# Turning q, k and x by DMA from chunk 14 instead of 18, with new planning numbers

## The chip, the cores and the metric

The kernel runs on one core of a Trainium2 chip. The metric is the time of one execution in microseconds (us) on the device. The core has TensorE (PE: matmuls; PEld: its weight loads), VectorE (DVE), ScalarE (ACT), GpSimd (POOL) and SyncE (SP, which here only issues DMAs), and 16 DMA engines that carry all transfers.

## What is computed

Gated linear attention runs over 4 batches x 8 heads x 768 steps with a head dimension of 48, and its output, as 3072 tokens of 384, goes through a two-layer MLP with a squared ReLU:

```python
for t in range(S):
    state = alpha[:, :, t, :, None] * state + np.einsum('bhd,bhe->bhde', k[:, :, t], v[:, :, t])
    y[:, :, t] = np.einsum('bhd,bhde->bhe', q[:, :, t], state)
...
h = x @ w_in
r = np.maximum(h, 0.0)
g = r * r
return (g @ w_out).astype(np.float32)
```

Inputs and outputs are float32; the kernel multiplies in bf16. w_in is 384 x 2048, w_out 2048 x 384.

## The kernel before, in words

The recurrence is cut into 24 chunks of 128 steps, 6 for each batch. For each chunk (`add_chunk`, from line 421) the kernel

- loads alpha, q, k and v (`at`, `qt`, `kt`, `vt`; line 362, on SP's queue, 192 KB each);
- takes logs of alpha (line 431, ACT), sums them along the chunk by a matmul with a triangular matrix, and exponentiates the sums: `A` or `Af` (line 459) and `Ainv` (line 463);
- multiplies q by A and k by 1/A (lines 487 to 493, DVE) into `qk_s`, which has four places, one for every fourth chunk;
- turns both, so that the head dimension lies on partitions: `qkT`;
- computes scores `sc` from `qkT`, masks them into `sm` (line 561), adds what comes from the state (`bank<-sb,qkT`) and from the chunk itself (`bank<-vb,sm`), and updates the state `st` (`st<-vb,qk_s`, then line 595);
- copies its output to bf16 (`xn`, line 388, ACT) and turns it into `xT_big`, the input of the MLP's first layer.

The first four chunks go through a version of their own (`add_super`). From chunk 8 on the scores of two chunks (8/9, 10/11, ...) are computed together.

There are two ways to turn. Up to a chunk `XFROM` (18) TensorE transposes: 8 matmuls with an identity for q and k and 3 for x (all line 269), into PSUM banks that the attention shares with the scores and the outputs; DVE then copies the result out (line 390, as `qkT` and `xT_big`; a few of the early ones go to ACT). From `XFROM` on SP issues one DMA transpose for q and k together (line 507, 256 KB with its padding) and one for x (line 409), from SBUF to SBUF. From chunk `TURN` (12) on, the chunk's decay factor `ae` (`ae_s`) is not computed by ACT, but taken from the last row of `Af` by two small DMAs that POOL issues (line 476).

The MLP works on groups of 4, 1, 1 and then 2 chunks (groups 6, 7 and 8 are the chunks 12/13, 14/15 and 16/17). The first layer (`bank<-xT_big,w_in_b`) is 16 x 3 matmuls for a group, with ReLU on ACT (line 866) and the square on DVE (line 874, `gT`); the second (`bank<-w_out_b,gT`) is 16 matmuls for each chunk. Results are copied out as `ob` (line 938) and stored on POOL's queue (line 947), those of the last three chunks on SP's.

The order of all this is written out by a planner in the file (`Plan`, line 63) when the program is built. Each piece of work is an `Op` with an engine, an assumed duration, a latency `lat` until its result may be used, and the pieces that it waits for; `Plan.run` lets time pass, each engine takes the piece that can start first (among equals the one with the lower `prio`), and the pieces are emitted sorted by planned start. Each engine then executes its list in just this order on the chip, and waits, by semaphores, where a result is not there yet. The planned times appear nowhere in the program, only the order does.

Four details of the planner matter here. A matmul that depends on another engine gets 0.05 us of slack after it, and 0.25 after planned time 25. Loads (engine "DMA") are planned first in, first out, with a duration and a latency of 2.4. From planned time `ISSUE_AT` on, everything that SP issues (loads, DMA transposes "XB", stores "OUT") also takes SP's time, 0.6 us or 1.25 for a transpose. And a gate holds a chunk's first matmul back until the MLP has come within `LEAD` (3.5) chunks of it; from chunk 12 on the lead grows by a quarter of a chunk per chunk, to 5.

Of the kernel before, what the change touches and what calls it, by code (L numbers as in the profile page):

```python
# [33 lines left out]
LAT = {"PE": 0.13, "ACT": 0.14, "DVE": 0.13, "POOL": 0.25}  # L34
PE_SLACK = 0.05
ISSUE = {"DMA": 0.6, "OUT": 0.6, "SPD": 1.2, "XB": 1.25}
ISSUE_AT = 75.0
PE_CALM = 25.0
PAUSES = [(13.0, 1.0), (18.0, 1.0)]

# [18 lines left out]
def after(op, x=0.0):  # L59
    return (op, x)  # L60


class Plan:
# [37 lines left out]
    def run(self, gate):  # L101
        free = self.free
        while any(self.pending.values()):
            best = None
            for eng, ops in self.pending.items():
                t0 = free.get(eng, 0.0)
                pick = None
                fifo = eng in ("DMA",)
                for op in (ops[:1] if fifo else ops):
                    if not gate(op):  # L110
                        continue
                    r = self.ready(op)
                    if r is None:
                        continue
                    if len(op.durs) > 1:
                        ends = {e: max(r, free.get(e, 0.0)) + x + LAT[e] for e, x in op.durs.items()}
                        if ends[eng] > min(ends.values()):
                            continue
                    key = (max(r, t0), op.prio)
                    if pick is None or key < pick[0]:  # L120
                        pick = (key, op)
                if pick is not None and (best is None or pick[0][0] < best[0]):
                    best = (pick[0][0], eng, pick[1])
            assert best is not None, "nothing can run"
            t, eng, op = best
            for e in op.durs:
                self.pending[e].remove(op)
            op.eng, op.dur = eng, op.durs[eng]
            op.start = t + getattr(op, "late", 0.0)
            if eng == "DMA" and self.pauses and t >= self.pauses[0][0]:  # L130
                op.dur += self.pauses.pop(0)[1]
            free[eng] = t + op.dur
            if op.lat is None:
                op.lat = LAT.get(eng, 0.2)
            if hasattr(op, "hold"):
                free["DMA"] = max(free.get("DMA", 0.0), t) + op.hold
            if hasattr(op, "dma"):
                free["DMA"] = max(free.get("DMA", 0.0), t) + op.dma
            if eng == "OUT":
                free["DMA"] = max(free.get("DMA", 0.0), t) + op.dur  # L140
            op.done = t + op.dur + op.lat
            if eng in ISSUE and t >= ISSUE_AT:
                sp = max(free.get("SPQ", 0.0), t)
                free["SPQ"] = sp + ISSUE[eng]
                op.start = max(op.start, sp)
                op.done = max(op.done, sp + ISSUE[eng] + op.lat)
                if eng == "DMA":
                    free[eng] = sp + op.dur
                    op.done = sp + op.dur + op.lat
            if op.takes is not None:  # L150
                self.ready(op)
                op.slot.release.append(op.gives if op.gives is not None else op)
            self.order.append(op)
            self.on_pick(op)
        self.order.sort(key=lambda o: o.start)
# [3 lines left out]
def kernel(  # L159
# [21 lines left out]
    NT = n_tok // P  # L181
# [64 lines left out]

    NBUF = 4
    TURN = 12
    AE_LAT = 3.0
    L_s = big.tile([P, NBUF, H, DP], BF16)  # L250
    nc.gpsimd.memset(L_s[:, :, :, D:], 0.0)
    qk_s = big.tile([P, NBUF, 2, H, DP], BF16)
# [9 lines left out]
    def pin(ins):  # L262
        tc.keep_in_program_order(ins)
# [4 lines left out]
    def tr(*a):  # L268
        pin(nc.tensor.transpose(*a))  # L269
# [11 lines left out]
    def psum(op, shape, dt):  # L281
        i = op.slot.bank
        return banks[i].tile(shape, dt, name=f"bank{i}")
    X_SLACK = 0.2
    LD = 1.05
# [4 lines left out]
    def add(eng, dur, emit, *deps, **kw):  # L290
        return plan.add(Op(eng, dur, emit, deps, **kw))
# [47 lines left out]
    SRC = dict(srcs)  # L339
    EARLY = 2 * 3  # L340
    PAIRS = 8
    XFROM, XTO = 18, NT
    XLAT = 2.8
    LEAD = 3.5

    NS = 2
# [6 lines left out]
    def add_load(s, nm):  # L353
        d = C[s]
        b, c = divmod(s, NCH)
        k = s // 2

        def ld():
            if s % 2 == 0:
                PAIR[k][nm] = loads.tile([P, 2, H, D], FP32, name=nm)  # L360
            d[nm] = PAIR[k][nm][:, s % 2]
            pin(nc.sync.dma_start(out=d[nm], in_=SRC[nm][b, c]))
        prev = C[s - LB]["use_" + nm] if s - LB >= 2 * NS else None
        if 2 * NS <= s < 2 * NS + LB and (k - LB // 2) < NS:
            prev = SUP[k - LB // 2]["use_" + nm]
        pace = C[s - LB + 1]["use_" + nm] if s >= TURN + 2 else None
        d["ld_" + nm] = add("DMA", LD if s < TURN else 0.97, ld, prev, pace, lat=2.4)

    PAIR = [dict() for _ in range(NT // 2)]
    SRC2 = [("at", alpha), ("qt", q), ("kt", k), ("vt", v)]  # L370
# [15 lines left out]
    def cast(op, out_t, in_t):  # L386
        if op.eng == "ACT":
            pin(nc.scalar.copy(out_t, in_t))  # L388
        elif op.eng == "DVE":
            pin(nc.vector.tensor_copy(out_t, in_t))  # L390
        else:
            pin(nc.gpsimd.tensor_copy(out_t, in_t))

    def add_tail(s, done, first, g):
        d = C[s]

        def e_xn():
            d["xn"] = work.tile([P, HD], BF16, name="xn")
            cast(xn, d["xn"], d["py"][:, 0:HD])
        xn = add("ACT", 0.36, e_xn, done, **g)  # L400
        first.gives = xn

        def e_p4():
            d["px"] = psum(p4, [P, KT, P], BF16)
            for j in range(KT):
                tr(d["px"][:, j, :], d["xn"][:, j * P:(j + 1) * P], ident_bf)
        if XFROM <= s < XTO:
            def e_xturn():
                pin(nc.sync.dma_start_transpose(out=xT_big[:, :, s * P:(s + 1) * P], in_=d["xn"]))
            d["x"] = add("XB", 0.0, e_xturn, xn, lat=XLAT - 0.9)  # L410
            d["end"] = xn
            return
        p4 = plan.add(Op("PE", 0.165, e_p4, [xn], takes=GLA_BANKS, lat=0.14, **g))

        def e_xT():
            cast(xT, xT_big[:, :, s * P:(s + 1) * P], d["px"])
        xT = add({"ACT": 0.36, "DVE": 0.27} if s < EARLY else "DVE", 0.27, e_xT, p4, prio=-9.0)
        d["x"] = d["end"] = xT
        p4.gives = xT

    def add_chunk(s):
        d = C[s]
# [48 lines left out]
        a_ = add("ACT", 0.38 if s < TURN else 0.76, e_A, p0, **g)  # L471
# [5 lines left out]
        if s < TURN:  # L477
            ae0 = add("ACT", 0.18, e_ae0, p0, after(ai), **g)
            p0.gives = ae1 = add("ACT", 0.19, e_ae1, p0, after(ae0), **g)
        else:  # L480
            p0.gives = ai
            ae1 = add("POOL", 1.8, e_aed, a_, lat=AE_LAT, prio=-20.0)
            ae1.dma = 0.3

        def e_qA():
# [26 lines left out]
        def e_cp(lo, hi):  # L512
            if lo == 0:
                d["qkT"] = work.tile([P, 2 * NP, P], BF16, name="qkT")
            cast(cpk if lo else cp, d["qkT"][:, lo:hi, :], d["pT"][:, lo:hi, :])
        if s < EARLY:
            cp = add({"ACT": 0.49, "DVE": 0.34}, 0, lambda: e_cp(0, NP), p1q, **g)
            cpk = add({"DVE": 0.34, "ACT": 0.49}, 0, lambda: e_cp(NP, 2 * NP), p1k, after(cp, -9.0), **g)
        elif s < XFROM:
            cp = cpk = add("DVE", 0.61, lambda: e_cp(0, 2 * NP), p1k, **g)  # L520
        else:
            cp = cpk = add("XB", 0.0, e_turn, mq, mk, lat=XLAT)
        if s < XFROM:
            p1q.gives = cpk

# [46 lines left out]
    def add_back(s):  # L572
# [47 lines left out]
        p3b = plan.add(Op("PE", 0.21, e_p3b, [after(sm1, 0.02), sm0, vb, after(p3a)], takes=None if c else GLA_BANKS, lat=0.15, **g))  # L620

        add_tail(s, p3b, p3a or p3b, g)

    def add_super(u):
# [209 lines left out]
    OUT_AT = 72.0  # L834
# [6 lines left out]
    prog = {"m1": 0.0, "m2": 0.0}  # L841
# [69 lines left out]
    def add_moe2(g, tt, before, box, quarters, pools):  # L911
# [3 lines left out]
        for qd in quarters:  # L915
# [8 lines left out]
            op = plan.add(Op("PE", 0.65, e_mm, deps, takes=pools if qd == 0 else None, prio=0.1))  # L924
# [14 lines left out]
        ev = add({"DVE": 0.47, "ACT": 0.38}, 0, e_ev, op, prio=-15.0)  # L939
        box["first"].gives = ev  # L940

        s = GT[g] + tt
# [6 lines left out]
                for t in range(2):  # L949
                    pin(q.dma_start(out=out2_r[s, t], in_=box["ob"][HF * t:HF * t + HF]))  # L950
        if s < NT - 3:
            add("POOL", 1.0, e_out, ev, at=OUT_AT + 3.0 * s, lat=2.5, prio=5.0).dma = 0.55
        else:
            add("OUT", 0.55, e_out, ev)
        return op
# [37 lines left out]
    def gate(op):  # L993
        s = getattr(op, "gla", None)
        if s is not None:
            return s <= (LEAD if s < 12 else min(5.0, LEAD + 0.25 * (s - 11))) + (prog["m1"] + prog["m2"]) / 5.12
        return True

    def on_pick(op):
        m = getattr(op, "moe", None)  # L1000
        if m:
            prog["m1" if m[0] == 1 else "m2"] += m[1]
    plan.on_pick = on_pick
    plan.run(gate)


# [47 lines left out]
```

## Time and profile before

| what | value |
| --- | --- |
| median of 3 runs | 181.76 us (181.5 to 182.21) |
| profiled execution, time | 181.87 us |
| profiled execution, span | 180.1 us |
| granted TensorE clock | 1.000 |
| scores of pairs 12/13, 14/15, 16/17, 18/19 start at | 92.2, 105.4, 115.6, 129.0 us |
| first-layer matmuls of groups 6, 7, 8, 9 start at | 98.5, 111.8, 122.2, 137.3 us |
| last matmul ends at | 177.4 us |

The span runs from the first to the last instruction that the profiler recorded; the execution's time is 1.8 us longer. All positions in this document are us from the start of the span. In a row of the profile a tile is written out<-in, with buffer numbers left out. The start of a DMA is the start of its issue, and "to landing" counts from there to the semaphore that tells of its end. A matmul's record lasts longer than the step from one matmul to the next, since they are pipelined; a piece of the chain counts the steps.

### The profile page before, as it was taken

What the parts mean: (1) busy time and instruction counts of PE and PEld (TensorE: products, weight loads), DVE (VectorE), ACT (ScalarE), POOL (GpSimd) and SP (SyncE); (2) the same over time, 40 slices, a digit from 0 to 9 for tenths busy, and PEclk for the clock granted to TensorE, in tenths of its full rate; (3) what the DMA queues carried; (4) which work ended last, traced back from release to release, by engine and by line L of the source; (5) the groups of instructions that cost most, each with busy time, mean ns of one, the idle gap of its engine ahead of it and who ended that gap; (6) DMA issues with size and microseconds to landing.
All of it is one profiled execution on the core that took longest, in us unless ns stands there. A gap on an engine that the chain in (4) does not pass through costs nothing.

```text
span 180.1 us, 4934 instructions
## 1 busy us (share of the span) xinstructions
PE 174.0 (97%) x1926; PEld 129.4 (72%) x1927; DVE 130.3 (72%) x269; ACT 122.4 (68%) x260; POOL 54.2 (30%) x95
## 2 busy tenths in 40 slices
PE   7799999999999999999999999999999999999993
PEld 3467684566996788866877887878767866868663
DVE  6699669847799889885999897997864971724300
ACT  4556879357997598937685967889577863657421
POOL 6023466612111116503643504543245022011100
PEclk9999999999999999999999999999999999999999
DMA  5999999999998989989999694596276325031022
GB/s 141 274 277 321 323 356 378 214 211 215 189 202 166 224 172 232 289 185 214 198 273 278 151 223 109 132 195 155 54 106 155 77 44 146 5 87 44 4 87 87
DMA packets 107799, 32.39 MB, mean 180 GB/s; under 512 B 101840, under 2 KB 106064, under 8 KB 107776
## 3 DMA queue, kind: packets, MB, share of 16 engines
q1 hardware_dynamic: 105536, 27.93, 70.3%
q0 software_dynamic: 2240, 4.15, 6.5%
q8 instruction: 15, 0.25, 0.6%
q14 instruction: 8, 0.07, 0.1%
HBM read 25.17 MB, written 4.72 MB: 166 GB/s over the span
## 4 chain that ended last, share of the span: by engine, by line
PE 87%; DVE 4%; ACT 3%; DMA 2%; issue 2%; SPq 1%; ACTq 0%; DVEq 0%
PE bank L266 77%; PE bank L269 5%; DMA at<-in_alpha_dram 2%; PE sc L266 2%; PE st L266 2%; ACT r L866 2%; DVE qkT L390 1%; DVE sm L753 1%; SPq L383 1%; DVE qk_s L690 1%; ACT xn L388 0%; DVE xT_big L390 0%; DVE qk_s L487 0%; ACT L_s L638 0%; ACT A L674 0%
## 5 line engine op out<-in xcount | busy, mean ns | idle before, releaser
L266 PE MATMUL bank<-xT_big,w_in_b 128*128 128x256 bf16 (+2 forms) x599 | 72.5, 268 | 0.2
L266 PE MATMUL bank<-w_out_b,gT 128*128 128x384 bf16 (+2 forms) x400 | 70.4, 319 | 0.0
L866 ACT ACTIVATE r<-bank 128x512 bf16<-128x512 f32 x96 | 56.8, 607 | 12.6 <-PE bank L266 10.4
L266 PEld LDWEIGHTS <-w_in_b 128*128 128x128 bf16 x600 | 52.9, 98 | 9.9 <-issue 0.3
L874 DVE TENSOR_TENSOR gT<-r 128x512 bf16<-128x512 bf16 x96 | 45.0, 500 | 13.4 <-ACT r L866 13.1
L266 PEld LDWEIGHTS <-gT 128*128 128x128 bf16 x400 | 36.9, 98 | 19.0
L436 POOL CAST vb<-vt 128x384 bf16<-128x384 f32 x20 | 12.0, 607 | 44.4 <-DMA vt<-in_v_dram 19.3
L938 ACT COPY ob<-bank 128x384 f32<-128x384 f32 x19 | 9.1, 481 | 17.6 <-PE bank L266 17.5
L947 POOL DMA_DIRECT2D out_dram<-ob x17 | 9.4, 555 | 33.1 <-ACT ob L938 31.2
L476 POOL DMA_DIRECT2D ae_s<-Af x24 | 12.2, 509 | 20.7 <-ACT Af L459 20.4
L561 DVE TENSOR_TENSOR sm<-sc,utri_b 128x512 bf16<-128x512 f32 x24 | 15.4, 687 | 2.8 <-PE sc L266 2.8
L388 ACT CAST xn<-bank 128x384 bf16<-128x384 f32 x24 | 11.2, 486 | 5.8 <-PE bank L266 5.6
L390 DVE COPY qkT<-bank 128x1024 bf16<-128x1024 bf16 (+1 forms) x20 | 12.4, 634 | 3.1 <-PE bank L269 2.9
L269 PE MATMUL bank<-ident_bf,qk_s 128*128 128x128 bf16 x144 | 13.0, 219 | 1.2 <-DVE qk_s L690 1.0
L266 PEld LDWEIGHTS <-qkT 64*128 64x128 bf16 (+2 forms) x304 | 10.5, 97 | 5.0 <-issue 2.2
L490 DVE TENSOR_TENSOR qk_s<-qt,Af 128x384 bf16<-128x384 f32 x12 | 10.3, 862 | 5.0 <-ACT Af L459 4.9
L269 PEld LDWEIGHTS <-qk_s 128*128 128x128 bf16 x144 | 9.7, 98 | 4.0 <-DVE qk_s L690 1.5
L459 ACT ACTIVATE Af<-bank 128x384 f32<-128x384 f32 x12 | 10.5, 873 | 2.2 <-issue 1.2
L493 DVE TENSOR_TENSOR qk_s<-kt,Ainv 128x384 bf16<-128x384 f32 x20 | 11.7, 587 | 0.1
L431 ACT ACTIVATE L_s<-at 128x384 bf16<-128x384 f32 x20 | 10.3, 527 | 1.5 <-DMA at<-in_alpha_dram 1.5
L595 DVE TENSOR_TENSOR st<-st,ae_s 128x384 f32<-128x384 f32 x16 | 9.0, 561 | 2.1 <-ACT xn L388 1.8
L463 ACT ACTIVATE Ainv<-bank 128x384 bf16<-128x384 f32 x20 | 10.3, 517 | 0.0
(71 smaller groups left out, 172.6 us busy)
## 6 DMA issues: line engine op xcount, KB each, us to landing
at<-in_alpha_dram SPq DMA_DIRECT2D x24, 192.0 KB, 4.0
qt<-in_q_dram SPq DMA_DIRECT2D x24, 192.0 KB, 4.1
kt<-in_k_dram SPq DMA_DIRECT2D x24, 192.0 KB, 4.1
vt<-in_v_dram SPq DMA_DIRECT2D x20, 192.0 KB, 3.9
out_dram<-ob POOLq DMA_DIRECT2D x17, 192.0 KB, 2.3
wo<-in_moe_w_out_dram SPq DMA_DIRECT2D x4, 768.0 KB, 7.4
wi<-in_moe_w_in_dram SPq DMA_DIRECT2D x4, 384.0 KB, 6.5
wi<-in_moe_w_in_dram SPq DMA_DIRECT2D x2, 768.0 KB, 5.2
```

What stands on the lines that cost most here:

```text
L266: pin(nc.tensor.matmul(*a, **kw))
L269: pin(nc.tensor.transpose(*a))
L388: pin(nc.scalar.copy(out_t, in_t))
L390: pin(nc.vector.tensor_copy(out_t, in_t))
L431: pin(nc.scalar.activation(L[:, :, 0:D], d["at"], AF.Ln))
L436: pin(nc.gpsimd.tensor_copy(d["vb"], d["vt"]))
L459: pin(nc.scalar.activation(d["A"], split(d["pm"][:, 0:HD], s), AF.Exp))
L476: pin(nc.gpsimd.dma_start(out=ae_s[HF * j:HF * j + D, i, j], in_=d["Af"][P - 1:P, j]))
L493: pin(nc.vector.tensor_mul(kI[:, :, 0:D], d["kt"], d["Ai"]))
L561: pin(nc.vector.tensor_mul(d["sm"][:, hh], d["sc"][hh], utri_b.to_broadcast([P, NP, P])))
L866: pin(nc.scalar.activation(box["r"][:, 0:w], box["ph"][:, 0:w], AF.Relu))
L874: pin(nc.vector.tensor_mul(gT[g][:, f0:f0 + per, lo * P:lo * P + n], r, r))
```

## The change

`XFROM` goes from 18 to 14, so the chunks 14 to 17 are turned by DMA too. In the planner, SP's issue time is counted from planned time 50 instead of 75; a transpose also occupies the planned DMA queue (`turn`, 0.9 for q and k, 0.4 for x), and is done no earlier than that queue; its latency goes from 2.8 to 2.2 (for x from 1.9 to 1.4). The factor DMAs are planned at 1.03 us on POOL and 2.0 us of latency instead of 1.8 and 3.0. Stores take 0.56 of POOL's time instead of 1.0. Loads from chunk 12 on are planned at 0.95 instead of 0.97. The lead grows from chunk 10 on instead of 12.

```diff
-ISSUE_AT = 75.0
+ISSUE_AT = 50.0
...
                 op.done = max(op.done, sp + ISSUE[eng] + op.lat)
+                if eng == "XB":
+                    free["DMA"] = max(free["DMA"], sp) + op.turn
+                    op.done = max(op.done, free["DMA"] + op.lat)
...
-    AE_LAT = 3.0
+    AE_LAT = 2.0
...
-    XFROM, XTO = 18, NT
-    XLAT = 2.8
+    XFROM, XTO = 14, NT
+    XLAT = 2.2
...
-        d["ld_" + nm] = add("DMA", LD if s < TURN else 0.97, ld, prev, pace, lat=2.4)
+        d["ld_" + nm] = add("DMA", LD if s < 12 else 0.95, ld, prev, pace, lat=2.4)
...
-            d["x"] = add("XB", 0.0, e_xturn, xn, lat=XLAT - 0.9)
+            d["x"] = add("XB", 0.0, e_xturn, xn, lat=XLAT - 0.8)
+            d["x"].turn = 0.4
...
-            ae1 = add("POOL", 1.8, e_aed, a_, lat=AE_LAT, prio=-20.0)
+            ae1 = add("POOL", 1.03, e_aed, a_, lat=AE_LAT, prio=-20.0)
...
             cp = cpk = add("XB", 0.0, e_turn, mq, mk, lat=XLAT)
+            cp.turn = 0.9
...
-            add("POOL", 1.0, e_out, ev, at=OUT_AT + 3.0 * s, lat=2.5, prio=5.0).dma = 0.55
+            add("POOL", 0.56, e_out, ev, at=OUT_AT + 3.0 * s, lat=2.5, prio=5.0).dma = 0.55
...
-            return s <= (LEAD if s < 12 else min(5.0, LEAD + 0.25 * (s - 11))) + (prog["m1"] + prog["m2"]) / 5.12
+            return s <= (LEAD if s < 10 else min(5.0, LEAD + 0.25 * (s - 9))) + (prog["m1"] + prog["m2"]) / 5.12
```

## The prediction

> **What bounds the kernel now.** I read the page first: the span, the share of each engine and the slices; then the waits of TensorE, the chain, the stretches of 10 us and the DMA issues.
>
> ```profile
> span 180.1 us, 4934 instructions
> ...
> PE 174.0 (97%) x1926; PEld 129.4 (72%) x1927; DVE 130.3 (72%) x269; ACT 122.4 (68%) x260; POOL 54.2 (30%) x95
> ...
> PE   7799999999999999999999999999999999999993
> ...
> PEclk9999999999999999999999999999999999999999
> DMA  5999999999998989989999694596276325031022
> ```
>
> TensorE is busy in 97% of the span, always at its full granted clock; no other engine passes 72%. The DMA engines are full until about 105 us, in the row's digits, and then have room. A busy matmul can hide a wait, so I also looked at starts: from one matmul to the next in the timeline, against the usual step of that kind. From 50 us to the end that leaves four waits, 0.20 us at 56.9, 0.12 at 66.8, 0.25 at 69.5 and 0.10 at 119.1: 0.67 us. So TensorE streams practically without gaps to 177.4, and its instruction time is the time.
>
> ```profile
> 43.70 0.61 PE bank L269 x11
> ...
> 97.11 0.61 PE bank L269 x11
> ...
> 153.45 23.94 PE bank L266 x214
> ```
>
> These are pieces of the chain of work that ended last (start, us, what). The first two are just what the change takes from a chunk: 8 transposes of q and k and 3 of x, 11 in all, on the path for 0.61 us. The third says that nothing in the tail waits.
>
> ```profile
> qkT<-qk_s SPq DMA_TRANSPOSE x6, 3.4
> xT_big<-xn SPq DMA_TRANSPOSE x6, 2.3
> ...
> ae_s<-Af POOLq DMA_DIRECT2D x24, 0.8 KB, 1.8
> ...
> 90.00:100.00 10.00, 10.00 (x117) 7.67 (x116) 9.01 (x19) 7.22 (x17) 3.74 (x8) 1.00 1.15 266
> 100.00:110.00 10.00, 10.00 (x126) 8.00 (x125) 9.92 (x20) 7.73 (x17) 3.96 (x8) 1.00 0.89 191
> 110.00:120.00 10.00, 10.00 (x122) 8.16 (x120) 8.92 (x20) 8.25 (x17) 3.52 (x7) 1.00 0.56 120
> 120.00:130.00 10.00, 10.00 (x98) 7.75 (x97) 8.07 (x19) 8.11 (x16) 3.94 (x7) 1.00 0.57 120
> ```
>
> First DMA issues with the median time to landing, then stretches: length, busy time of PE, PEld, DVE, ACT and POOL, clock, DMA share, GB/s. The DMA turns exist already, for chunks 18 to 23; what matters is how long they take, and that the chunks which now join them (14 to 17) work between 85 and 122 us, half in full DMA traffic and half not.
>
> **The change, part by part.**
>
> *Removed from TensorE.* Chunks 14 to 17 lose 11 transposes each: 4 x 0.61 = 2.44 us, all on the path. VectorE also loses the copies of these results, 4 x (0.68 + 0.36) = 4.2 us, and the two banks that the transposes held are free sooner. VectorE is off the path, so I count that as nothing.
>
> *Added to SP and the DMA engines.* Eight DMA transposes. Their issue takes 1.28 us (q and k) and 1.20 (x) on SP: 4 x 2.48 = 9.9 us of SP. In the packets of the trace one q/k turn is 1024 packets of 256 bytes, 21.9 us summed over the 16 engines (the turn of 124.3), one x turn 384 packets and 7.5. So 4 x 29.4 / 16 = 7.4 us of all engines. From 100 to 130 us the shares 0.89, 0.56 and 0.57 leave, below the 1.15 seen as full, 2.6 + 5.9 + 5.8 = 14.3 us: it fits. Queued behind a turn's wait on SP are loads, and they have time: alpha of chunk 18 lands at 92.4 and is read at 110.1, that of chunk 20 lands at 101.4 and is read at 121.1, k of 23 lands at 124.0 and is read at 148.1. I cost late loads at nothing; a load would have to lose 10 us before it counts.
>
> *The longer latency.* For chunk 15 the path over TensorE takes from the end of the k product (101.35) to the end of the copy (103.22), 1.9 us; a turn takes 3.4. For x it is 1.1 us (110.25 to 111.37) against 2.3. So the pair's x comes some 2.7 us later, and the first matmul of its MLP group, now at 111.78, with it. Its cover is second-layer work: the first layer of the group before ends at 106.9, and the two output tiles that it feeds, 2.6 us each, run only from 118.1 and 127.6. 5.2 us of cover for 2.7; and the scores of 14/15 start at 105.42, 2.2 us after the copy, so part of it is absorbed there. Without the cover it would cost up to 2.7 us a pair, 5.4 us.
>
> *The planner's new numbers.* TensorE's order is written out ahead, so a landing that comes later than planned is a wait of TensorE itself. Two are trimmed:
> - Factors by DMA: planned 1.8 + 3.0 + 0.25 (slack) = 5.05 us from the POOL issue to the state matmul, now 1.03 + 2.0 + 0.25 = 3.28. Measured from the first issue to the second landing, chunks 12 to 16, in full traffic: 4.94, 4.65, 3.49, 2.62, 3.93; later chunks 2.0 to 3.4. Only chunk 12 has nothing else to wait for: issue 84.01, landing 88.95, matmul 89.00. The others wait for the state before them. So TensorE waits there between 0 (at 2.62) and 1.66 us (at 4.94). I take the median of the five, 3.93: **0.65 us**; the nearest row in time would give 1.66, which I keep for the range.
> - Turns: planned 1.25 + 2.8 + 0.25 = 4.3 us, now 3.7 for q and k, or later by the planned DMA queue. Measured 3.1 to 3.4, and once 4.5. Only the second turn of a pair counts. That of 17 falls where the DMA engines are idle (k product ends at 113.6): 0. That of 15 starts at about 101.4 among loads, which there take 2.8 to 4.0; from 0 (a turn at 115.87, among loads, took 3.33) to 0.8 (the 4.5). I take **0.4**. The x turn is planned at 2.9 and measured at 2.3 to 2.4: 0, up to 1.0 if traffic adds to it what the 4.5 shows.
>
> *The rest.* Modelling SP's issue from 50 us on instead of 75, loads at 0.95, stores and factors with shorter POOL times and the looser gate (chunks from 10 on may start up to half a chunk sooner) move work about, but issue no more of it. A new order may lose the old 0.67 us of waits or find as many others: nothing, with -0.6 to +0.6 for the range.
>
> *Sum,* against the profiled execution (181.87 us, of which 180.1 is span and 1.8 lies around it): -2.44 + 0.65 + 0.4 = -1.39, so 180.48. The median shown is 0.11 below that execution: **180.4 us**, 0.8% below 181.76.
>
> *What the skill says against it.* The Trainium skill, "VectorE: DVE Perf Modes", section "The three transpose paths", gives 390 ns for a 128x128 bf16 transpose on TensorE and 1309 ns by DMA, and its section "Rules for kernel authors" says to use TensorE where a PSUM destination will do. Read as cost, 11 transposes would by these figures be 4.3 us on TensorE and 14.4 by DMA, an estimate from that page, 10.1 us a chunk against the change. The row above says otherwise for a stream: 0.61 us for the 11, so the page's TensorE figure is not the step that TensorE pays here, and a DMA turn is off TensorE altogether.
>
> **The rivals.**
> 1. *Waits eat the gain (same).* The factor wait is 1.66, the turn of 15 costs 0.8 and another such comes at an x turn or at 17: 2.44 - 1.66 - 0.8 = nothing left, 181.8, and up to 182.4 with 0.6 of further waits. For it: the 4.94 at just the chunk that is not covered. Against it: four of five factor landings were quicker.
> 2. *Slower: turns land behind loads.* The mechanism is one: the pair 14/15 meets full DMA traffic, and its turn takes as long as the slowest load of that stretch, 6.1 us (q of chunk 14, 70.7 to 76.8), against 3.7 planned: 2.4 us of waiting at the scores; its x turn, 5.0 (a load's 6.1 less the 1.1 by which an x turn is shorter) against 2.9, 2.1 more. -2.44 + 4.5 = +2.1, so 183.8. It decides once such waits pass 2.44 + 0.91 = 3.35 us in sum. For it: the stretch from 90 to 100 has a DMA share of 1.15. Against it: a turn among loads took 3.33, and the turn that ends the wait comes after 101 us.
> 3. *The change doesn't bite:* the cover is used up, TensorE waits for x at 14 to 17 and ends when it ended: 181.8. Against it: the pairs from 18 on run by DMA turns now, and between 120 and 177 TensorE shows no wait at all.
>
> The Trainium skill's rule just cited ("VectorE: DVE Perf Modes", section "Rules for kernel authors") would have the outcome of the second rival; the stretch from 120 us on, with turns and without a wait, speaks against it.
>
> **How the numbers follow.** Faster by over 0.5% means below 180.85, slower above 182.67; 0.5% is about what a measurement of this kernel can tell from no change. My forecast with its neighbourhood up to 180.85: 0.64. Rivals 1 and 3 together, within 0.5%: 0.21. Rival 2: 0.15. Range: down to 181.76 - 2.44 - 0.6 = 178.7, say 178.8 (no new wait, the old ones gone); up to 181.76 - 2.44 + 1.66 + 0.8 + 0.8 = 182.6 (factor wait and a turn's wait in each pair at their upper ends). That leaves rival 2 outside.
>
> **What the new profile would show.** Right: 112 transposes of q and k and 42 of x on TensorE instead of 144 and 54; 10 DMA turns of each kind; TensorE's last matmul near 176; a wait of some 0.6 us before the state matmul of chunk 12 and a small one before the scores of 14/15; turns of 3 to 4.5 us. Wrong: turns of 5 us or more, TensorE waiting for the qkT or xT_big landings by over 1 us each, first-layer matmuls of chunks 14 to 17 with TensorE idle before them, or loads landing after they were wanted.

## The result, and the profile after

The kernel became **slower**: its median is 187.96 us (186.04 to 188.88, 4 runs), against 181.99 us (181.5 to 182.3, 4 runs) of the kernel before, measured beside it; the ratio is 1.030 (95% interval 1.023 to 1.037). The forecast was 180.4 us. Medians here are over all executions, while ratios leave out disturbed ones (the core at a lower granted clock, or more than 1.5% above the shortest execution of the same kernel), so the two can differ.

The traced execution of the kernel after took 186.04 us, of which 184.2 is span: 4.1 us more than the span before. First the rows of its page that answer to those shown of before.

```profile
span 184.2 us, 4856 instructions
...
PE 174.3 (95%) x1882; PEld 127.2 (69%) x1883; DVE 125.0 (68%) x260; ACT 123.0 (67%) x261; POOL 52.8 (29%) x95
...
PE   7799999999999999999999994999999999999994
...
PEclk9999999999999999999999998899999999999999
DMA  5999999799899979999789999999999424120022
```

The row PE now has a 4 at about 111 us, PEclk has two 8s from there on, and the digits of DMA stay at 9 until 140 us, where before they fell away from 105. The list of TensorE's waits of over 0.15 us (total, times, longest, in us) names what is new:

```profile
PE bank L269 <- DMA xT_big<-xn: 3.2, 3, 2.6
```

Lines are shifted by 3 to 5: 269 is the matmul helper, 272 the transposes, 365 the loads, 412 the turn of x, 511 the turn of q and k. Before, no DMA was in this list. TensorE's timeline around 111 us (start, us, then the row; in brackets idle time before it and what ended it) and SP's shortly before:

```profile
108.00 3.09 PE L269 MATMUL bank<-w_out_b,gT 128*128 128x384 bf16 x18
110.93 0.33 PE L269 MATMUL bank<-L_s,utri_b 128*128 128x384 bf16 x1
113.88 4.38 PE L269 MATMUL bank<-xT_big,w_in_b 128*128 128x256 bf16 x25 [2.62 <-DMA xT_big<-xn]
```

```profile
102.43 2.60 SPq L511 DMA_TRANSPOSE qkT<-qk_s  x1
105.08 0.58 SPq L365 DMA_DIRECT2D qt<-in_q_dram  x1
105.70 0.58 SPq L365 DMA_DIRECT2D kt<-in_k_dram  x1
106.38 2.06 SPq L412 DMA_TRANSPOSE xT_big<-xn  x1
108.49 0.58 SPq L365 DMA_DIRECT2D vt<-in_v_dram  x1
109.17 2.53 SPq L412 DMA_TRANSPOSE xT_big<-xn  x1
```

The first row is second-layer work, 18 of 28 such matmuls that run one behind the other from 106.38 on. Then the MLP group of chunks 14 and 15 waits for its two x turns. That of 14 is issued at 106.38, and its issue alone holds SP for 2.06 us (before, 1.20). By the packet records its first packet moves at 108.63, its last ends at 111.57, and it lands at 112.25, 5.87 us after the issue. The issue of the turn of 15, whose input was there at 107.14, comes only at 109.17, behind the first turn and a load; it lands at 113.83. The tile's landing times show it is no single case. The row of after, and then the row of before:

```profile
DMA to landing us min/median/max: 2.3/3.9/5.9
```

```profile
DMA to landing us min/median/max: 2.3/2.3/2.4
```

What else was in flight? The DMA view of 106 to 114 us of after has a row that the same view of before's first x turns (132 to 137) lacks:

```profile
q8 instruction: 1, 0.02, 0.7%
```

Its columns are packets, MB and the share of the 16 engines' time. It is a fetch of instructions, one packet of 16 KB that takes from 108.94 to 109.88, in the middle of that turn. The page counts 14 of them; in the packet records they come about every 250 TensorE instructions, and four of the five pairs that are turned in the kernel after (fetches at 108.94, 123.68, 137.53, 149.57) have one in their x turns: 5.87 and 4.67 us, 4.09 and 3.54, 4.35 and 3.74, 4.06 and 3.37. The last pair has none, and takes 2.36 and 2.34. In the kernel before the fetches (120.7, 130.9, 144.1, 156.4) missed the packets of every x turn; the last reached 0.3 us into the issue of the turn at 156.98, which landed after 2.36 all the same.

**The account.** I took the step from one matmul's start to the next, less the usual step of its kind, summed over the trace, as in the prediction. The sum of such excess is 11.2 us after and 4.9 before. The wait at 110.93 is 2.79 of it; the 13 matmuls right behind it step at 213 instead of 109 ns, at half the clock, 1.36; three more waits for x (126.8, 140.3, 152.6) make 1.09; the first 30 us 0.6, though the order on every engine is the same up to 70 us; small ones elsewhere the rest. Against 6.3 us more of waiting stand the 2.44 of transposes that left TensorE: 3.9 of the 4.1 us. The three executions of the kernel after without a trace took 1.9 to 2.8 us more than the traced one. Why is open, so the account covers the 4.1 us of the traced execution and not the 6 us between the medians.

### The profile page after: what moved, and what is told of

It is laid out like the page before. It is cut to its first block, busy times and chain, and to the rows that moved or that the text cites. A ratio compares the mean times of both kernels' runs of the same rounds, so it can differ in the third digit from the quotient of the medians.

```text
span 184.2 us, 4856 instructions
## 1 busy us (share of the span) xinstructions
PE 174.3 (95%) x1882; PEld 127.2 (69%) x1883; DVE 125.0 (68%) x260; ACT 123.0 (67%) x261; POOL 52.8 (29%) x95
## 4 chain that ended last, share of the span: by engine, by line
PE 74%; DMA 10%; SPq 5%; ACT 4%; DVE 3%; issue 2%; POOL 1%; DVEq 0%; ACTq 0%
PE bank L269 67%; DMA xT_big<-xn 6%; SPq L386 5%; DMA vt<-in_v_dram 4%; PE bank L272 3%; PE sc L269 2%; PE st L269 2%; ACT r L871 2%; DVE sm L566 1%; ACT xn L391 1%; DVE qk_s L497 1%; DVE xT_big L393 1%; POOL vb L651 1%; ACT L_s L435 0%; DVE qk_s L491 0%
## 5 line engine op out<-in xcount | busy, mean ns | idle before, releaser
L269 PE MATMUL bank<-xT_big,w_in_b 128*128 128x256 bf16 (+2 forms) x599 | 73.9, 272 | 3.5 <-DMA xT_big<-xn 3.2
L269 PE MATMUL bank<-w_out_b,gT 128*128 128x384 bf16 (+2 forms) x400 | 69.0, 319 | 0.0
L879 DVE TENSOR_TENSOR gT<-r 128x512 bf16<-128x512 bf16 x96 | 42.9, 480 | 18.8 <-ACT r L871 18.6
L440 POOL CAST vb<-vt 128x384 bf16<-128x384 f32 x20 | 10.9, 543 | 50.8 <-DMA vt<-in_v_dram 29.0
L943 ACT COPY ob<-bank 128x384 f32<-128x384 f32 x20 | 9.6, 479 | 16.6 <-PE bank L269 16.4
L393 DVE COPY qkT<-bank 128x1024 bf16<-128x1024 bf16 (+1 forms) x16 | 9.7, 619 | 3.4 <-PE bank L272 3.4
L272 PE MATMUL bank<-ident_bf,qk_s 128*128 128x128 bf16 x112 | 10.1, 219 | 1.4 <-DVE qk_s L695 1.0
L566 DVE TENSOR_TENSOR sm<-bank,utri_b 128x512 bf16<-128x512 f32 x16 | 10.2, 680 | 0.0
```

The source lines that it names most:

```text
L269: pin(nc.tensor.matmul(*a, **kw))
L440: pin(nc.gpsimd.tensor_copy(d["vb"], d["vt"]))
L566: pin(nc.vector.tensor_mul(d["sm"][:, hh], d["sc"][hh], utri_b.to_broadcast([P, NP, P])))
L879: pin(nc.vector.tensor_mul(gT[g][:, f0:f0 + per, lo * P:lo * P + n], r, r))
```

## The experiments

My theory after the result was that a turn among loads is late, and that a fetch makes it later. Rivals: the planner merely plans the turns too early, so that a true latency would cure it; the loss comes from the planner's other numbers; SP, standing at a turn, holds back the loads.

### Which part of the change costs?

**e2_move_only**, the kernel before with only the first DMA turn moved:

```diff
-    XFROM, XTO = 18, NT
+    XFROM, XTO = 14, NT
```

> The kernel before with XFROM 14 and none of the new planning numbers. Numbers theory: the move is good alone, 179.5 to 180.5 us. Traffic theory: x is planned 0.5 us later than in the changed kernel, so waits are smaller by that, 185 to 187. Fetch theory: it depends on where the fetches fall; x turns that meet one take 3.4 us or more, those that meet none below 3.3, and the time goes with the number of meetings: 181 with none, 185 with one at 14/15.

Measured: 184.53 us against 182.01, ratio 1.015 (1.008 to 1.022). Its TensorE waits for q and k (1.22 us at 105.5), for x (1.37 at 116.4, and 0.75) and, at 111.0, for 0.88 us that the profile puts down not to a turn but to ScalarE's copy `xn`. The move alone loses; a theory that blames the planner's numbers alone falls.

**e3_numbers_only**, the kernel after with the first turn moved back:

```diff
-    XFROM, XTO = 14, NT
+    XFROM, XTO = 18, NT
```

> The changed kernel with XFROM back at 18, so only the planner's numbers differ from before. Numbers theory: most of the loss stays, 185 to 188. Traffic and fetch theory: the loss goes with the turns of 14 to 17; within 1 us of before, 181 to 183, unless a fetch now meets the x turns of 18 to 23, which would show as x turns over 3.4 us.

Measured: 183.06 us, ratio 1.006 (1.004 to 1.008). The numbers cost about 1 us by themselves, without any new turn.

**e10_move16**, the kernel before with two chunks more instead of four:

```diff
-    XFROM, XTO = 18, NT
+    XFROM, XTO = 16, NT
```

> The kernel before with XFROM 16: only the pair 16/17 joins the DMA turns, with the old planning numbers. 1.2 us of TensorE saved. Loads: four more transposes push them back by some 6 us instead of 16 or more, so the turns of 20 and later are in calm traffic again. If pushed-back loads are the main trouble the waits are about half of those of the full move (1.5 of 3.9 us beyond the savings): 181.5 to 183. If already the first pair among loads costs all, 184 or more.

Measured: 184.17 us against 182.08, ratio 1.010 (1.007 to 1.013). Already the first pair that moves among the loads waits, 1.29 us for x (the turn of 17 took 3.4, with loads and without a fetch); the next pair, which went by DMA before too, waits 0.79 for q and k.

**e11_factor_only**, the kernel before with only the factor DMAs' numbers of the kernel after:

```diff
-    AE_LAT = 3.0
+    AE_LAT = 2.0
...
-            ae1 = add("POOL", 1.8, e_aed, a_, lat=AE_LAT, prio=-20.0)
+            ae1 = add("POOL", 1.03, e_aed, a_, lat=AE_LAT, prio=-20.0)
```

> The kernel before with only the factor DMAs planned shorter (1.03 and 2.0 us instead of 1.8 and 3.0). The prediction's term: TensorE waits 0.65 us (0 to 1.66) for the factor at the state matmul of chunk 12, so 182.0 to 183.6. If the factor lands in time, or the matmul waits for something else first, no change, 181.5 to 182.3, and the 1 us that the new numbers cost without the move has another source.

Measured: 183.29 us, ratio 1.006 (1.004 to 1.008): all that e3 loses. But the wait is not TensorE's: its state matmul of chunk 12 starts at 87.47, before the factor lands at 88.96. VectorE's product with the factor waits. The timeline of VectorE in e11, then in the kernel before:

```profile
89.08 0.57 DVE L595 TENSOR_TENSOR st<-st,ae_s 128x384 f32<-128x384 f32 x1 [0.30 <-DMA ae_s<-Af]
```

```profile
89.87 0.57 DVE L595 TENSOR_TENSOR st<-st,ae_s 128x384 f32<-128x384 f32 x1
```

The new plan puts this product 0.8 us sooner, and it stands 0.30 us for its factor with the rest of VectorE's work queued behind. TensorE then waits at 92.2, 94.6, 105.8 and 108.2, 1.1 us in all, for other work of VectorE and ScalarE. That those four come from the 0.30 is argued from their order, not shown.

**e4_x_on_tensor**, the kernel after with q and k turned from 14 on, x only from 18:

```diff
-        if XFROM <= s < XTO:
+        if XFROM + 4 <= s < XTO:
```

> The changed kernel, but x of chunks 14 to 17 still goes over TensorE (q and k by DMA from 14). Both the fetch and the traffic theory hold x turns for the culprit: the wait of 2.8 us ahead of the first layer of 14/15 and the half clock go, 4 x 0.17 = 0.7 us of TensorE come back: 181 to 182.5. If the turns of q and k are the trouble (waits before the scores of 14/15 and 16/17): 185 to 188.

Measured: 184.23 us against 182.01, ratio 1.010 (1.006 to 1.015). Its waits:

```profile
PE bank L269 <- DMA qkT<-qk_s: 1.6, 2, 0.8
...
PE bank L269 <- DMA xT_big<-xn: 0.9, 2, 0.6
```

With the four x turns gone, the next late turns carry the wait: q and k at 102.4 and 128.5, x of later chunks.

### Is it only planned too early, or SP's standing?

**e5_long_latency**, the kernel after with turns planned as late as they landed:

```diff
-    XLAT = 2.2
+    XLAT = 3.8
...
-            d["x"] = add("XB", 0.0, e_xturn, xn, lat=XLAT - 0.8)
+            d["x"] = add("XB", 0.0, e_xturn, xn, lat=XLAT - 0.4)
```

> The changed kernel, with the planned latency of a q/k turn at 3.8 instead of 2.2 and of an x turn at 3.4 instead of 1.4: done 5.05 and 4.65 us after the planned issue, as the traced turns among loads (3.4 to 5.9). If the loss is that results land later than TensorE's fixed order allows for, the waits for turns (4.4 us of them, with 1.4 us of half clock behind the largest) go down to those that a fetch makes longer than planned, under 1.5 us in all, with second-layer work in between: 181 to 183.5. If the later x is what hurts, because there is no other work to put ahead, TensorE waits elsewhere (first layer, for x) and the time stays at 185 to 188.

Measured: four executions, 184.31 us (the traced one) and 188.7 to 190.3; no ratio comes out of them. Even the shortest is 2 us behind the kernel before. The waits for turns are gone from its list, and others stand there:

```profile
PE bank L269 <- DVE sm L566: 1.2, 1, 1.2
PE bank L269 <- ACT r L871: 1.2, 1, 1.2
```

Planning later moves the wait; I read this as too little other work to put under the latency, which the trace does not show by itself. e8, below, comes out the same with a ratio. "Only planned too early" falls.

**e12_loads_first**, the kernel after with SP's q and k turns held back, so that loads are issued ahead of them:

```diff
+            cp.late = 3.0
```

> The changed kernel with each q/k turn put 3 us later in SP's list than planned, that is behind the next two or three loads. If SP standing at a turn (4.0 us for that of chunk 14 alone) is what pushes the loads back, the loads of chunks 17 to 19 are issued 3 us or more sooner and the last load lands near 135 instead of 142.5; turns whose k product was there in time are issued some 2 us later, so q/k waits grow. In sum no better than the changed kernel: 185 to 188. If SP's standing still does not matter, loads land as in the changed kernel.

Measured: 185.71 us, ratio 1.022 (1.015 to 1.028). The q of chunk 17 is loaded 6 us sooner, but the last load lands at 141.6 instead of 142.5 (before: 124.7), and x still costs 2.7 us of waiting. So with q and k turns held back the last load comes hardly sooner. What stays the same is the time that turns hold SP while they are issued: the first ten, 17.3 us in the kernel after, 1.2 to 2.6 each, and 16.9 here. That this pushes the loads back more than SP's standing is argued, not shown.

### Loads and instruction fetches apart

**e1_phase114**, the kernel after with 64 narrow matmuls in place of the warm-up, 114 TensorE instructions more, so that all fetches come sooner:

```diff
-    idle_mm(7, 4)
+    def narrow_mm(n):
+        wp = banks[4].tile([P, 512], FP32, name="bank4")
+        for _ in range(n):
+            mm(wp[:, 0:48], lhsT=warm, rhs=warm[:, 0:48], start=True, stop=True)
+
+    narrow_mm(64)
```

> The changed kernel, with the 7 wide idle matmuls at its start replaced by 64 narrow ones (48 columns) of about the same total time: 114 more instructions (matmuls and weight loads) ahead of everything else on TensorE, order otherwise the same. In the trace of the changed kernel a 16 KB instruction fetch comes with every 256 TensorE instructions, and at four of five pairs it falls into the x turns, whose packets then stand still for about 1 us. Fetch theory: moved some 5.6 us ahead, the fetches miss the x turns, these take 2.3 to 3.3 us instead of 3.4 to 5.9, the wait of 2.8 us for x of chunk 14/15 shrinks below 0.7, the 3 us at half clock behind it go: about 181 us. Traffic theory (turns are late because loads fill the DMA engines): turns and waits as in the changed kernel, 186 to 188. Numbers theory (the planner's new, shorter latencies are at fault): the same 186 to 188.

Measured: 184.37 us against 182.01, ratio 1.011 (1.007 to 1.015). The fetches move to 104.85, 117.59, 132.62 and 144.92, and its x turns land in

```profile
DMA to landing us min/median/max: 2.3/3.1/3.8
```

The order on the other engines is unchanged, and no stretch at half clock is left. Shifting the fetches alone takes back 3.6 of 6 us, by the medians; the waits that remain are for x (0.83 and 1.42 us) and q and k (0.62 twice).

**e6_light_loads**, the kernel after with the loads of chunks 14 to 23 read in runs of 1536 bytes instead of 192:

```diff
+    RUN = {n: a.rearrange("b h s d -> (b h s) d").rearrange("(c p r) d -> c p r d", p=P, r=H) for n, a in srcs}
...
-            pin(nc.sync.dma_start(out=d[nm], in_=SRC[nm][b, c]))
+            pin(nc.sync.dma_start(out=d[nm], in_=RUN[nm][s] if s >= 14 else SRC[nm][b, c]))
```

> The changed kernel, but the loads of chunks 14 to 23 read the same number of bytes in contiguous runs of 1536 bytes instead of 192: other elements of the inputs, so this kernel computes something else there, with the same work. The packets of a load fall from 1024 to 128 or so and its time on the DMA engines to about half (a store of the same size takes some 8 us summed over the engines, a load 16). The order on every engine stays that of the changed kernel. Traffic theory: with the loads out of the way turns start 1.2 us after their issue and land in 3.0 to 3.5 (q, k) and 2.3 to 2.6 (x), apart from those that meet a fetch; the waits at 14/15 and 18 to 21 fall below 1 us in all: 180 to 182. Fetch theory alone: x turns still meet fetches in the same places, waits of 1 to 2.5 us stay: 183 to 186.

Measured: 184.9 us against 182.05, ratio 1.015 (1.011 to 1.019). Six of the ten q and k turns come down to 3.0 to 3.4 us; the x turns, into which the fetches still fall, do not:

```profile
DMA to landing us min/median/max: 2.4/3.9/4.8
```

```profile
PE bank L270 <- DMA xT_big<-xn: 2.5, 3, 1.7
```

**e9_light_phase**, both edits together.

> The changed kernel with both the contiguous loads of chunks 14 to 23 (other elements of the inputs, so this kernel computes something else there, with the same work; half the time on the DMA engines) and the 114 more narrow matmuls and weight loads at the start that move the fetches. Each alone took some 3 us off the loss. If load traffic and fetches are the two causes of late turns, x turns take 2.3 to 2.6 us and q/k turns 3.0 to 3.6 except where a fetch now meets one of the latter, waits for turns stay below 0.8 us in all, and the time falls to 181 to 182.5, the removed transposes showing against the 1 us of the other numbers. If something else delays turns, 184 to 185 as with either alone.

Measured: 181.87 us against 182.08, ratio 0.998 (0.995 to 1.001). No turn is in the list of TensorE's waits any more, and the stretches of 10 us (length, busy time of five engines, clock, DMA share, GB/s) have TensorE full at full clock. First e9, then the kernel after:

```profile
110.00:120.00 10.00, 10.00 (x113) 7.74 (x111) 6.36 (x14) 7.37 (x15) 2.87 (x6) 1.00 0.96 219
```

```profile
110.00:120.00 10.00, 7.38 (x61) 5.25 (x60) 3.75 (x8) 4.39 (x8) 2.06 (x4) 0.83 0.99 185
```

With both lessened the loss of the full change is gone; with one alone 1.1 to 1.5% stay. The share of all DMA work in the rows above hardly differs (0.96 and 0.99): from 100 to 120 us the load packets fall from 10550 to 1518, their share of the 16 engines' time only from 0.62 to 0.44. Which of the two matters to a turn, the number of packets or their time, is not separated.

**e7_calm_fetch**, the kernel before, its turns unmoved and in calm traffic, with 202 TensorE instructions more (72 narrow matmuls at the start, narrower ones as filler), so that fetches fall into its turns. How many filler matmuls stand between the early pieces is worked out from planned times, the one place where these reach the program:

```diff
-    idle_mm(7, 4)
+    narrow_mm(72)
...
-                idle_mm(n // 2, 4)
+                fill_mm(n // 2)
```

> The kernel before, in which the x turns of 18 to 23 come in calm traffic, take 2.3 us and meet no fetch. Its idle matmuls in the first 20 us are replaced by more, narrower ones, 202 more TensorE instructions, so fetches come about 9.5 us sooner: near 134.5, 147 and 159, into the x turns. Fetch theory: x turns that meet a fetch take 3.3 to 4.3 us instead of 2.3, with packets that stand for up to 1 us, and the time rises by up to 1 us, as their results had 1.1 to 1.6 us in hand. Traffic theory without the fetch: 2.3 us throughout and no change of time.

Measured: 183.43 us against 182.05, ratio 1.007 (1.003 to 1.010). The x turns, all 2.3 to 2.4 before, now take 3.58 and 2.53, 2.92 and 2.85, 3.25 and 3.11 us, without loads about. The first of each pair has the fetch in it, and its issue alone takes 2.26, 1.82 and 2.07 us instead of 1.2. So a fetch lengthens a turn. The second has none in it; beside the last two of these run packets of a store, which may be why they are late. It is not the whole of the 1.4 us: TensorE waits for x only 0.21 and 0.20, and two waits at 57.97 (0.85) and 70.2 (0.57) come ahead of all turns.

Over the 18 traces of this document the x turns sort by what shared their time ("loads": more than 200 load packets from issue to last packet; "a fetch": between the turn's first packet and its landing; packet time is from first to last packet):

| x turns | number | landing, min/median/max us | median packet time, us |
| --- | --- | --- | --- |
| neither loads nor a fetch | 81 | 2.28/2.36/4.85 | 0.63 |
| loads only | 38 | 2.33/3.38/4.67 | 0.76 |
| a fetch only | 20 | 2.86/3.75/4.7 | 1.55 |
| both | 19 | 3.05/4.29/5.87 | 1.61 |

Loads put a turn's start off (1.0 us more to landing, packets hardly longer), a fetch stretches the packets themselves. For q and k the medians to landing are 3.44, 4.0, 4.44 and 5.18. The first row holds 20 turns whose issue, though not their packets, met a fetch: their median is 3.14, that of the other 61 is 2.35. Of these 61, the 13 that met a store's packets have 2.79, the other 48 have 2.35.

**e8_long_phase**, e5 and e1 together.

> The changed kernel with both the longer planned latencies of turns (5.05 and 4.65 us) and the 114 more narrow matmuls and weight loads at the start that move the fetches. If late landings (traffic and fetch) are the whole loss beyond the about 1.1 us that the planner's other numbers cost alone, 2.4 us of removed transposes show: 180 to 182, with waits for turns under 0.8 us in all. If not, 183 to 185 as with the moved fetches alone.

Measured: 186.76 us, ratio 1.026 (1.022 to 1.029): a clear miss. With long planned latencies TensorE waits for other work (ScalarE's r 2.3 us, VectorE's sm 1.4, ScalarE's sb 0.9), wherever the fetches fall.

### With the old numbers for the factors

**e16_oldfactor**, the kernel after with the factor DMAs planned as before:

```diff
-    AE_LAT = 2.0
+    AE_LAT = 3.0
...
-            ae1 = add("POOL", 1.03, e_aed, a_, lat=AE_LAT, prio=-20.0)
+            ae1 = add("POOL", 1.8, e_aed, a_, lat=AE_LAT, prio=-20.0)
```

> The changed kernel with only the factor DMAs planned as before (1.8 and 3.0 us). With the fetches moved this was worth 1.9 us (184.4 to 182.4). If the factor's share stands by itself, 186 here, with the wait for x of 14/15 still there; if the shifted order lets the x turns miss the fetches, 183 to 184; if the wait for x hides the factor's share, 187 to 188.

Measured: 183.89 us against 182.34, ratio 1.007 (1.004 to 1.010). So taking back the factor numbers takes back some 4 us of the full change, though alone they cost 1.2: shares do not add. The order shifts, the x turns of 14 and 15 are issued at 105.2 and 106.6 and land at 109.1 and 109.8, ahead of the fetch at 111.8. TensorE waits 1.12 us there instead of 2.79, and later fetches still meet turns (0.99, 0.63, 0.46).

**e13_phase_oldfactor** (e16 and e1) and **e14_light_phase_oldfactor** (e16, e6 and e1):

> The changed kernel with the fetches moved (64 narrow matmuls at the start) and the factor DMAs planned as before (1.8 and 3.0 us). If the factor's shorter plan costs its 1.2 us here too, 184.3 becomes 183.1; if the waits that late turns cause cover it, 184 to 184.5. Faster than the kernel before only if both causes were nearly gone, which the load traffic speaks against.

> The changed kernel with contiguous loads of chunks 14 to 23 (other elements of the inputs, so it computes something else there, with the same work), the fetches moved, and the factor DMAs planned as before. If load traffic, fetches and the factor's plan are all that stands against the 2.4 us of removed transposes, these show now: 180.0 to 181.0. If the transposes' time does not come back even then (another engine bounds), 181.5 to 182.3 as with the factor's new plan.

Measured: e13 182.44 us, ratio 1.003 (1.001 to 1.005), with 1.12 and 1.19 us of waiting for x; e14 181.52 us against 182.13, ratio 0.999 (0.996 to 1.001). In e14 no turn is in the list of waits, and its last matmul ends at 176.5 (before, 177.4): of the 2.44 us saved 0.9 arrives in the traced execution. Of the rest 0.9 goes in the first 30 us, and some 1 us, most of it in waits for VectorE and ScalarE, between 82 and 130 us. No version clearly beats the kernel before.

**e15_move_phase**, e2 with the narrow matmuls of e1:

> The kernel before with XFROM 14, its own planning numbers, and the 64 narrow matmuls at the start that move the fetches. Without them the move alone took 184.5, with waits for turns of 3.9 us of which one x turn of four and two q/k turns had met a fetch. If fetches make half of those waits, 182.5 to 183.5; if load traffic makes nearly all of them, 184 to 185.

Measured: 183.47 us against 182.34, ratio 1.005 (1.002 to 1.008), against 1.015 of e2: the fetches' part of the move alone is about 1%, or most of its loss. Its eleven executions spread from 182.61 to 187.74 us, and the traced one took 186.83: there TensorE waits 3.4 us for x from 115.7 on, and the record has half clock from 118.3 to 125.1. So this trace says nothing about the ratio.

## Why the prediction was wrong

- **Right: what leaves TensorE.** Transposes fell from 144 and 54 to 112 and 42, and the account closes with the 2.44 us. No gain from VectorE's relief shows.
- **Right in part, but given 0.15: the mechanism of the second rival.** Turns of the early pairs do land late among loads, and TensorE waits for them; it put 183.8 us, and the kernel took 187.96. It knew nothing of the fetch, and it looked for the larger wait at the scores; in the kernel after it is at x (e4 has it at the scores).
- **Failed: "The x turn is planned at 2.9 and measured at 2.3 to 2.4: 0, up to 1.0".** This is the step that decided. The x turns of 14 and 15 took 5.87 and 4.67 us, and TensorE waited 2.79 for them, with 1.36 lost at half clock behind it; the later pairs' x made 1.09 more. The second-layer cover that I had counted was there, 28 matmuls from 106.38 to 110.93, and it was used up by then, 2.9 us before the turn of 15 landed. The range did not even hold this 1.0: with one such x wait in each pair, and the +0.6 that I had named for the rest, its upper end would have been 185.2, still below 187.96. My rows were six turns in calm traffic; the table of four cases above says what a turn costs elsewhere, and one of the two causes, the fetch, I had not thought of. A row of before showed it: the q/k turn of 4.47 us at 128.92, which I read as traffic, had a fetch at 130.9 in it. e9 shows that the loss goes when both causes are lessened, e1 and e6 that either alone leaves a part, e7 that a fetch alone lengthens a turn. How much of the loss is each one's stays open, since e16 takes back 4 us with loads and fetches both still about.
- **Failed: "I cost late loads at nothing".** I priced a late load by its own reader. No wait of TensorE after 30 us is put down to a load, so far that held (POOL's casts of v did wait, 29.0 us in all against 19.3); but the alpha of chunk 20 is issued at 111.7 instead of 96.6, and the last load lands at 142.5 instead of 124.7, so that the DMA share from 110 to 140 is 0.99, 1.00 and 1.13 where it was 0.56, 0.57 and 0.71. The displaced loads meet the turns of 16 to 20; that of 17 I had put into idle traffic. The cost of the issues was mis-sized in the same part: 9.9 us of SP for the eight turns, measured 14.8, with up to 2.6 us for one.
- **Wrong: the waits of 0.65 us for the factor and 0.4 for the q and k turn of 15.** The factor's new numbers cost 1.2 us alone (e11), but the wait for it is VectorE's, 0.30 us ahead of the state product; none of TensorE's waits is put down to it. The turn of 15 took 3.60 us, and TensorE shows no wait for it.
- **Failed: "The rest ... nothing, -0.6 to +0.6".** A new order also decides which turns a fetch meets: e16 and the kernel after differ by 4 us through two planned numbers. I had no term for that.

The rule of the Trainium skill that I weighed ("VectorE: DVE Perf Modes", section "Rules for kernel authors") pointed the right way, though not by its prices: 11 transposes do take 0.61 us in the stream, the saving on TensorE came as counted, and the loss came from the turns' landing.

## What to carry to other kernels

Take a DMA's time to landing from transfers that met the traffic into which it will be moved, and if there are none, let the range say so. A load that is pushed back harmlessly for its own reader is not free: ask what it will then be in flight beside. In an order written out ahead, a saving of 2.4 us of instructions is worth only what waits of one late landing leave of it, and planning a latency as long as it really is did not help here (e5, e8), since TensorE then waited for other work.

## What the runs showed of the hardware

- **An instruction fetch stalls a DMA transpose.** With one fetch of 16 KB, about 1 us long, the packet time of an x turn more than doubles in the median (0.63 to 1.55 us without loads); at worst, with loads about, it was 2.94 us. In the kernel after 20 packets of loads (192 bytes) that start between 109.87 and 110.24, just as the fetch of 108.94 ends, took 1.2 to 1.6 us each instead of about 15 ns. In all 18 traces 505 packets of at most 512 bytes took over 0.8 us after 60 us; 496 of them overlap a fetch or start within 1.5 us of its end. The Trainium skill, "Runtime: NRT & Kernel Launch", section "Instruction fetch mechanics", says that instructions are refilled in 16 KiB blocks of 256, at a cost mostly hidden. The block size agrees with the trace (0.23 MB in 14 fetches, one per some 250 TensorE instructions); hidden it is for TensorE (none of the four waits of the kernel before after 50 us falls into a fetch), but not for the turn beside it.
- **2.6 us of idling were followed by half clock, 2.1 were not.** After the wait of 2.62 us in the kernel after the granted clock of the stretch is 0.83; after one of 2.10 us at 133.4 in e8 it stays at 1.00. The Trainium skill, "TensorE: Matmul & The Clock Gate", section "Part 1: The HAM clock gate", gives an idle window of about 3.4 us; here less was enough.
- **The issue of a turn is not constant, and a fetch lengthens it too.** For x it held SP for 1.18 to 1.27 us in the 68 turns with neither loads nor a fetch in the issue. Among loads the median stays at 1.21 (44 turns, up to 2.06); with a fetch in the issue and no loads it is 1.82 (33 turns, up to 2.64). For q and k loads alone do it: 1.25 in calm traffic, 1.65 among loads (76 turns, up to 2.81).
